# Two transformer-like MLP layers after an attention: the second layer's first product in a Strassen form

## The chip, the cores and the metric

One core of one Trainium2 chip. The metric is device time in microseconds (us) of one execution, as the median of a few executions. TensorE is PE in the rows, VectorE is DVE, ScalarE is ACT, GpSimd is POOL; SP is SyncE, which here only starts DMAs.

## The reference

```python
def _attn_ref(x, state):                                  # x 4x8x512x64, state 4x8x32x64
    a  = softmax(scale * x @ state.T);     xread = a @ state     # 512 tokens of each batch
    a2 = softmax(scale * state @ x.T);     sread = a2 @ x        # 32 state rows of each batch
    return np.concatenate([xread, sread], axis=2)
def _moe_ref(x, w_in, w_out):                             # layer 1: ELU
    h = x @ w_in                                          # 512 -> 2048
    return np.where(h > 0, h, np.exp(np.minimum(h, 0)) - 1) @ w_out   # 2048 -> 512
def _moe2_ref(x, w_in, w_out):                            # layer 2: mish
    h = x @ w_in
    sp = np.where(h > 20, h, np.log1p(np.exp(np.minimum(h, 20))))
    return (h * np.tanh(sp)) @ w_out
```

The attention gives 4·(512 + 32) = 2176 rows of 512, which both layers take one after the other. The weights come as 64-bit floats and are converted on the chip.

## The kernel before

**Precision.** A product is taken to float32 accuracy with three fast matmuls: each operand is split into a rounded high part and the rest (`copy` and a subtraction), and high·high, high·low and low·high are added in PSUM (L756 to L758, L836 to L838).

**Tokens.** 17 tiles of 128: four batches of four tiles, and a last tile with the 4·32 state rows. A *step* is one block of tokens and one block j of 128 of the 2048 features: its first product (`mm1`) fills a PSUM bank `h`, `hidden` makes g of it on ACT and DVE, and `mm2`, two steps later, multiplies g by w_out into accumulators `acc`. Layer 1 takes a batch (512 tokens) at a time, steps (1, b, j); its last batches add their second half of features to results that lie in DRAM as x2d, loaded again as `half` (L889), added, and written back (L896). Layer 2 has five blocks of 4, 4, 3, 3 and 3 tiles (`BLOCKS2`), steps (2, blk, j): 12 matmuls of n·128 columns, then n·3 of 512 columns.

**Mish** of a tile is a chain over two engines: exp on ACT (L775), minimum (L792) and u = e·(e+2) (L793) on DVE, Ln (L795) and exp (L796) on ACT, two products (L797, L798) on DVE, then the high part (L800, ACT) and the rest (L801, DVE).

**Weights of layer 2** are converted during layer 1 (L453 to L478), written to DRAM (`w2d`, L481), loaded again when layer 1 ends (`reload`), and split (L500). `load_x2` loads and splits a block of layer 2's input.

**Order.** `Plan` keeps a list of operations with costs, data dependences and due times, and fixes every engine's order before the kernel runs: each engine executes its list strictly in that order, each DMA too is started in the order of its queue's list. PSUM has the banks `h` (two), `att` (two) and `acc0` to `acc3`.

## Time and profile before

| | |
|---|---|
| median of 3 runs | 743.83 us (743.46 to 744.91) |
| the profiled execution: time, and its span in the trace | 744.95 us, 743.2 us |
| TensorE busy over the span | 723.5 us, 3874 matmuls |
| VectorE / ScalarE busy | 532.1 us / 448.0 us |
| share of the last chain that is TensorE's | 95% |
| start of layer 2's first matmul | 355.2 us |

The span is what the trace covers; the time of an execution is 1.75 us more. Matmuls overlap, so a matmul's own duration is longer than its share of the engine: what counts is the distance from one start to the next.

### The profile page before, as it was taken

How to read it: one execution, taken by the hardware profiler on the slowest of the kernel's cores; microseconds unless marked ns; L12 is line 12 of the kernel's file. 1: busy time of each engine (PE TensorE's matmuls, PEld its weight loads, DVE VectorE, ACT ScalarE, POOL GpSimd, SP SyncE). 2: the span in 40 equal slices, each digit the busy share in tenths (PEclk: the TensorE clock that was granted, in tenths of full speed). 3: DMA queues.
4: the chain of work that ended last, by engine and by line, in shares of the span. 5: the costliest groups of instructions: out<-in, count | busy, mean ns of one | idle time of the engine just before them, and what ended most of it. 6: DMA issues, size and time to landing. Idle time of an engine off the chain costs nothing.

```text
span 743.2 us, 10373 instructions
## 1 busy us (share of the span) xinstructions
PE 723.5 (97%) x3874; PEld 580.2 (78%) x3874; DVE 532.1 (72%) x955; ACT 448.0 (60%) x796; POOL 2.7 (0%) x14
## 2 busy tenths in 40 slices
PE   4899999999999999999999999999999999999996
PEld 3345777776777779878888888888899999989894
DVE  6889988768478884687899856575567566666553
ACT  4687787656388673777767645454545455555443
POOL 0000000000000000000000000000000000000000
...
GB/s 226 280 174 64 119 158 201 41 142 1 159 161 156 91 202 56 200 241 180 254 185 231 44 0 100 1 0 1 6 94 1 1 86 1 1 1 43 1 1 42
DMA packets 48090, 73.28 MB, mean 99 GB/s; under 512 B 5544, under 2 KB 28840, under 8 KB 48040
## 3 DMA queue, kind: packets, MB, share of 16 engines
...
q10 hardware_dynamic: 2212, 0.66, 0.4%
...
## 4 chain that ended last, share of the span: by engine, by line
PE 95%; DVE 2%; ACT 1%; DMA 1%; issue 0%; ACTq 0%
PE acc_acc L836 16%; PE acc_acc L838 15%; PE acc_acc L837 15%; PE h L756 12%; PE h L758 12%; PE h L757 12%; PE acc_acc L824 3%; PE h L742 2%; PE fold L535 2%; PE h L732 2%; DMA st_raw<-in_state 1%; PE xT L601 1%; PE sr L684 1%; PE acc_att L837 0%; PE acc_att L836 0%; PE acc_att L838 0%
## 5 line engine op out<-in xcount | busy, mean ns | idle before, releaser
L775 ACT ACTIVATE e<-h 128x512 f32<-128x512 f32 (+1 forms) x148 | 83.2, 562 | 129.6 <-PE h L758 117.9
L800 ACT CAST g<-e 128x512 fp32r<-128x512 f32 (+1 forms) x142 | 82.4, 580 | 61.7 <-PE acc_acc L838 31.6
L801 DVE TENSOR_TENSOR g<-e,g 128x512 fp32r<-128x512 f32 (+1 forms) x142 | 91.2, 642 | 28.7 <-ACT g L800 27.9
L838 PE MATMUL acc_acc<-w_out,g 128*128 128x512 f32 x272 | 106.9, 393 | 0.0
L837 PE MATMUL acc_acc<-w_out,g 128*128 128x512 f32 x272 | 106.7, 392 | 0.0
L836 PE MATMUL acc_acc<-w_out,g 128*128 128x512 f32 x272 | 105.9, 389 | 0.4 <-ACT g L800 0.4
L836 PE MATMUL acc_acc<-g,w_out 128*128 128x512 f32 x232 | 93.3, 402 | 0.0
L838 PE MATMUL acc_acc<-g,w_out 128*128 128x512 f32 x232 | 90.6, 391 | 0.0
L837 PE MATMUL acc_acc<-g,w_out 128*128 128x512 f32 x232 | 90.4, 390 | 0.0
L797 DVE TENSOR_TENSOR u<-u,e 128x384 f32<-128x384 f32 (+1 forms) x80 | 48.9, 611 | 54.0 <-ACT e L796 53.9
L795 ACT ACTIVATE e<-u,two 128x384 f32<-128x384 f32 (+1 forms) x80 | 52.8, 660 | 49.4 <-DVE u L793 49.3
L792 DVE TENSOR_SCALAR e<-e 128x384 f32<-128x384 f32 (+1 forms) x80 | 30.9, 386 | 51.6 <-ACT e L775 51.6
L785 DVE SCALAR_TENSOR_TENSOR e<-e,h 128x512 f32<-128x512 f32 x62 | 42.3, 683 | 27.3 <-ACT e L778 27.2
L838 PEld LDWEIGHTS acc_acc<-w_out,g 128*128 128x128 f32 x272 | 51.1, 188 | 11.0 <-DVE g L801 0.3
L836 PEld LDWEIGHTS acc_acc<-w_out,g 128*128 128x128 f32 x272 | 51.1, 188 | 10.1 <-ACT g L800 0.9
L837 PEld LDWEIGHTS acc_acc<-w_out,g 128*128 128x128 f32 x272 | 51.0, 188 | 9.5
L836 PEld LDWEIGHTS acc_acc<-g,w_out 128*128 128x128 f32 x232 | 43.6, 188 | 18.4 <-issue 6.3
L758 PE MATMUL h<-x,w_pair 128*128 128x384 f32 (+1 forms) x160 | 57.3, 358 | 0.0
L758 PE MATMUL h<-x,w_in 128*128 128x384 f32 (+1 forms) x160 | 57.3, 358 | 0.0
L756 PE MATMUL h<-x,w_pair 128*128 128x384 f32 (+1 forms) x160 | 57.3, 358 | 0.0
L756 PE MATMUL h<-x,w_in 128*128 128x384 f32 (+1 forms) x160 | 57.3, 358 | 0.0
L757 PE MATMUL h<-x,w_in 128*128 128x384 f32 (+1 forms) x160 | 57.2, 357 | 0.0
(135 smaller groups left out, 1324.1 us busy)
## 6 DMA issues: line engine op xcount, KB each, us to landing
raw_out<-in_moe_w_out SPq DMA_DIRECT2D x32, 512.0 KB, 3.8
raw_in<-in_moe_w_in SPq DMA_DIRECT2D x32, 256.0 KB, 5.9
raw_in<-in_moe_w_in SPq DMA_DIRECT2D x16, 512.0 KB, 4.1
w2d<-wv SPq DMA_DIRECT2D x32, 256.0 KB, 3.0
xb<-in_x SPq DMA_DIRECT2D x16, 256.0 KB, 5.2
x2d<-o SPq DMA_DIRECT2D x16, 256.0 KB, 3.9
back_in<-w2d SPq DMA_DIRECT2D x16, 256.0 KB, 2.8
back_out<-w2d SPq DMA_DIRECT2D x16, 256.0 KB, 2.9
```

The costliest lines, as they stand in the source:

```text
L756: nc.tensor.matmul(h[:, :n], lhsT=wh, rhs=xh, start=(k == 0), stop=False)
L757: nc.tensor.matmul(h[:, :n], lhsT=wh, rhs=xl, start=False, stop=False)
L758: nc.tensor.matmul(h[:, :n], lhsT=wl, rhs=xh, start=False, stop=(k == nk - 1))
L775: add("ACT", act(n), lambda: nc.scalar.activation(E(), Hh(), AF.Exp), r=[h], w=[e])
L785: add("DVE", dve(n), lambda: nc.vector.scalar_tensor_tensor(E(), E(), -1.0, Hh(), ALU.mult, ALU.max), r=[e, h], w=[e])
L795: add("ACT", act(n) + 0.12, lambda: nc.scalar.activation(E(), U(), AF.Ln, bias=two), r=[u, "two"], w=[e])
L797: add("DVE", dve(n), lambda: nc.vector.tensor_tensor(U(), U(), E(), ALU.mult), r=[u, e], w=[u])
L800: add("ACT", act(n) + 0.01, lambda: nc.scalar.copy(g[:, 0, :n], E()), r=[e], w=[(g, 0)])
L801: add("DVE", dve(n), lambda: nc.vector.tensor_tensor(g[:, 1, :n], E(), g[:, 0, :n].bitcast(F32), ALU.subtract), r=[e, (g, 0)], w=[(g, 1)])
L836: nc.tensor.matmul(acc.t, lhsT=st[:, 0, :], rhs=mv[:, 0, :], start=fst, stop=False)
L837: nc.tensor.matmul(acc.t, lhsT=st[:, 0, :], rhs=mv[:, 1, :], start=False, stop=False)
L838: nc.tensor.matmul(acc.t, lhsT=st[:, 1, :], rhs=mv[:, 0, :], start=False, stop=lst)
```

## The change

Layer 2's 16 full tiles are taken in two halves m of 1024 tokens, and the features in eight pairs p of blocks. In each the first product is a 2×2×2 product of half-blocks (512 tokens, 128 features, 256 of the depth) in Strassen-Winograd form: seven half-block products of 6 matmuls of 512 columns (`product`, L1009 of the changed kernel), instead of eight. It needs

- sums of halves of w_in2 (`combine`, in layer 1: per pair four half-width sums, four high parts, four rests, eight DMAs to `wi2d`), loaded per pair (`load_pair`);
- four sums of layer 2's input and seven splits (`load_x2`), once per half;
- per pair three copies of a PSUM bank to SBUF on ACT (`out_of`, L1021: p1, u2, u3), and three sums of such a copy and a bank on DVE (`plus`: c11, and the two late blocks).

Of a pair's four blocks (two of features, two of 512 tokens) the two of the first 512 tokens get their mish and second product at once. The two of the second 512 tokens wait in SBUF as `late`; their mish follows the pair's own (for pairs 5 to 7 all together behind pair 7), and their second product comes after the pairs, 16 blocks at 12 matmuls. The state rows (last tile) lose their own block: in each pair of the second half, 12 matmuls of 256 columns (`last_tokens`), and later 16 transposes and 48 matmuls. w_out2 is converted at the end of layer 1 and in the first pairs of layer 2 (`last_weight`) and no longer goes through DRAM. The loads of `half` now come after the first product of the step in which they are placed, and the first products are chained in their order.

```diff
-BLOCKS2 = [(0, 4), (4, 4), (8, 3), (11, 3), (14, 3)]
+NP = NF // 2
+EITHER_LATE = 0.5
+BEHIND = 0.0
+PUT_OFF = 5
...
-    w2d = pools["dram"].tile([P, 2, NF, DM], F32, name="w2d")
+    wi2d = pools["dram"].tile([P, NP, 4, 2, 2, 2 * P], F32, name="wi2d")
...
+    def last_weight(j):
+        raw = buf("work", "wraw", 3, [P, DM], I64, f"raw_out2_{j}_")
+        y = buf("work", "wy", 2, [P, DM], F32, f"last_y{j}_")
+        v = buf("work", "wv", 2, [P, DM], F32, f"last_v{j}_")
+        r = lambda i: raw.t.bitcast(U32).rearrange("p (f t) -> p f t", t=2)[:, :, i]
+        add(SP, 512.0, lambda: nc.sync.dma_start(out=raw.t, in_=w_dram[2][1][j * P:(j + 1) * P, :]), w=[raw],
...
+    def combine(p, a1, a2):
+        tt(lambda: sb[:, lo], lambda: a2[:, lo], lambda: a2[:, hi], ALU.add, [a2], [(sb, 0)])
+        tt(lambda: sa[:, lo], lambda: sb[:, lo], lambda: a1[:, lo], ALU.subtract, [a1, (sb, 0)], [(sa, 0)])
+        tt(lambda: sa[:, hi], lambda: a1[:, lo], lambda: a2[:, lo], ALU.subtract, [a1, a2], [(sa, 1)])
+        tt(lambda: sb[:, hi], lambda: a1[:, hi], lambda: sa[:, lo], ALU.subtract, [a1, (sa, 0)], [(sb, 1)])
...
+        for i, v in enumerate((a1, a2, sa, sb)):
+            r = [v] if i < 2 else [(v, 0), (v, 1)]
+            h, l = (buf("work", "o", OBUFS, [P, DM], F32R, f"comb{p}_{i}_{q}_") for q in range(2))
+            add(EITHER, {"ACT": 0.61, "DVE": 0.43}, lambda e, v=v, h=h: copy(e, h.t, v.t), r=r, w=[h], place=[l])
+            add("DVE", 0.69, lambda v=v, h=h, l=l: nc.vector.tensor_tensor(l.t, v.t, h.t.bitcast(F32), ALU.subtract),
+                r=[*r, h], w=[l])
+            for q, t in enumerate((h, l)):
+                add(SP, 256.0, lambda i=i, q=q, t=t: nc.sync.dma_start(
+                    out=wi2d[:, p, i // 2 * 2:i // 2 * 2 + 2, i % 2, q, :], in_=t.t.bitcast(F32).rearrange("p (s f) -> p s f", s=2)),
+                    r=[t], w=[("wi2d", p, i, q)])
...
+                add(SP, 256.0, lambda o=o, rows=rows: nc.sync.dma_start(out=o.t, in_=rows), r=names, w=[o], lag=2.0,
+                    after=[step_op[s]])
...
+        load("b12", 0, 1)
+        load("b11", 0, 0)
+        load("b22", 1, 1)
+        load("b21", 1, 0)
+        minus("t1", "b12", "b11")
+        split("b11")
+        minus("t2", "b22", "t1")
+        minus("t3", "b22", "b12")
+        split("t1")
+        minus("t4", "b21", "t2")
+        split("b21")
+        split("t2")
+        split("t4")
+        split("t3")
+        split("b22")
+        x2_done[:] = [plan.writer[sums["t4"]]]
...
+    def load_pair(m, p):
+        pair_t[m, p] = [buf("w", "w_in", NF // 2, [P, 2, 2, 2 * P], F32R, f"pair{m}_{p}_{i}_") for i in range(4)]
+        for i, t in enumerate(pair_t[m, p]):
+            n = (m * NP + p) * 4 + i
+            add(SP, 512.0, lambda i=i, t=t: nc.sync.dma_start(out=t.t.bitcast(F32), in_=wi2d[:, p, i]),
+                             r=[("wi2d", p, i // 2 * 2 + g, q) for g in range(2) for q in range(2)], w=[t], lag=1.0,
+                after=[last_use[n - 6]] if n >= 6 else x2_done if n >= 4 else folded)
+
+
+    PRODUCTS = [(0, 0, "b11"), (1, 0, "b21"), (2, 0, "t2"), (2, 1, "t1"), (3, 0, "t3"), (1, 1, "t4"), (3, 1, "b22")]
+
+    put_off = []
...
+    def mish(H, keys, dst, wkeys, after=()):
+
+
+        e = buf("work", "e", EBUFS, [P, MAXN])
+        u = buf("work", "vu", 2, [P, MAXN], F32, "u")
+        add("ACT", act(S), lambda: nc.scalar.activation(e.t, H(), AF.Exp), r=keys, w=[e], after=after)
+        add("DVE", 0.43, lambda: nc.vector.tensor_scalar(e.t, e.t, E20, None, ALU.min), r=[e], w=[e])
+        add("DVE", 0.69, lambda: nc.vector.scalar_tensor_tensor(u.t, e.t, 2.0, e.t, ALU.add, ALU.mult), r=[e], w=[u])
+        add("ACT", act(S) + 0.12, lambda: nc.scalar.activation(e.t, u.t, AF.Ln, bias=two), r=[u, "two"], w=[e])
+        add("ACT", act(S) + 0.03, lambda: nc.scalar.activation(e.t, e.t, AF.Exp, scale=-1.0), r=[e], w=[e])
+        add("DVE", 0.69, lambda: nc.vector.tensor_tensor(u.t, u.t, e.t, ALU.mult), r=[u, e], w=[u])
+        if dst is None:
+            add("DVE", 0.69, lambda: nc.vector.tensor_tensor(e.t, H(), u.t, ALU.mult), r=[*keys, u], w=[e])
+            return high_low(lambda: e.t, [e])
+        add("DVE", 0.69, lambda: nc.vector.tensor_tensor(dst(), H(), u.t, ALU.mult), r=[*keys, u], w=wkeys)
+
+    def high_low(src, keys):
+        g = buf("work", "g", GBUFS, [P, 2, MAXN], F32R, "g")
+        turn_[:] = [add("ACT", act(S), lambda: nc.scalar.copy(g[:, 0, :], src()), r=keys, w=[(g, 0)], after=turn_)]
+        add("DVE", 0.69, lambda: nc.vector.tensor_tensor(
+            g[:, 1, :], src(), g[:, 0, :].bitcast(F32), ALU.subtract), r=[*keys, (g, 0)], w=[(g, 1)])
+        return g
+    def pair(m, p, due, late):
...
+        ps = [buf("ps", t, 2, [P, MAXN], F32, f"prod{m}_{p}_") for t in ("h", "att", "att")]
...
+        def product(q, bank, fst, lst):
+            n, pos, name = PRODUCTS[q]
+            w, x = parts[n], X[name]
+
+            def f():
+                for k in range(2):
+                    c = slice(k * P, (k + 1) * P)
+                    for i, (a, b) in enumerate(((0, 0), (0, 1), (1, 0))):
+                        nc.tensor.matmul(bank.t, lhsT=w[:, pos, a, c], rhs=x[b][:, k, :],
+                                         start=fst and k == i == 0, stop=lst and k == 1 and i == 2,
+                                         skip_group_check=not fst)
+
+            chain[:] = [add("PE", 6 * mm(S), f, r=[w, part(x[0], 0), part(x[1], 0)], w=[bank],
+                            due=due[q], after=chain)]
+            last_use[(m * NP + p) * 4 + n] = chain[0]
+
+        def plus(o, a, bank, r, w):
+            add("DVE", 0.69, lambda: nc.vector.tensor_tensor(o(), a.t, bank.t, ALU.add), r=[a, bank, *r], w=w)
+
+        def out_of(o, bank):
+            add("ACT", act(S), lambda: nc.scalar.copy(o.t, bank.t), r=[bank], w=[o], after=converted)
+
+        end = p == NP - 1
+        product(0, ps[0], True, True)
+        out_of(P1S, ps[0])
+        product(1, ps[1], True, True)
+        plus(lambda: C11.t, P1S, ps[1], [], [C11])
+        product(2, ps[0], False, True)
+        out_of(U2, ps[0])
+        if m:
+            last_tokens(p, due[7])
+        if not end:
+            product(3, ps[2], True, True)
+        product(4, ps[0], False, True)
+        out_of(U3, ps[0])
+        if end:
+            product(5, ps[0], False, True)
+            product(3, ps[2], True, True)
+        plus(lambda: L(1), U3, ps[2], [], [B_[1]])
+        if not end:
+            product(5, ps[0], False, True)
+        product(6, ps[2], False, True)
+        plus(lambda: L(0), U2, ps[2], [], [B_[0]])
+        g = [mish(lambda: C11.t, [C11], None, None), mish(lambda: ps[0].t, [ps[0]], None, None)]
+        for e in range(2):
+            put_off.append((L, e, B_[e]))
+        if p < PUT_OFF or end:
+            first = chain if end else ()
+            for L, e, b in put_off:
+                mish(lambda e=e, L=L: L(e), [b], lambda e=e, L=L: L(e), [b], after=first)
+            put_off.clear()
+        return g
...
+        for m in range(2):
...
+                todo = [[p, e, i, 0.0] for e in range(2) for i in range(NC)]
+            moved[m] = chain[0]
+            if not m:
+                load_x2(1)
+                load_x16()
+            block = 2 * NC * m
+            for i in range(NC):
+                for e in range(2):
+                    d = tick(C3)
+                    out_mm(g[NP - 1][e], NF - 2 + e, slice(i * P, (i + 1) * P), A_(i), False, e == 1, d)
+                result(block + i, A_(i), d, 0)
+            if m:
+                last_out(tick)
+            accB = [buf("ps", t, 2, [P, MAXN], F32, f"accB{m}_{i}_") for i, t in enumerate(("att", "att", "h", "h"))]
+            gB = [None] * NF
+            for j in range(NF):
+                gB[j] = high_low(lambda t=late[m, j]: t[0][:, t[1], :], [late[m, j]])
+                if j < NF - 2:
+                    for i in range(NC):
+                        out_mm(gB[j], j, slice(i * P, (i + 1) * P), accB[i], j == 0, False, tick(C3), chain)
+            for n, i in enumerate((2, 3, 0, 1)):
+                for j in (NF - 2, NF - 1):
+                    d = tick(C3)
+                    out_mm(gB[j], j, slice(i * P, (i + 1) * P), accB[i], False, j == NF - 1, d)
+                if not n:
+                    chain[:] = [plan.ops[-1]]
+                result(block + NC + i, accB[i], d, 0 if not m else 2 if n == NC - 1 else 1)
...
+    def last_tokens(p, due):
...
+        def f():
+            for k in range(NK):
+                w, c = halves[k // 2], slice(k % 2 * P, (k % 2 + 1) * P)
+                for i, (a, b) in enumerate(((0, 0), (0, 1), (1, 0))):
+                    nc.tensor.matmul(bank[:, :2 * P].rearrange("p (s f) -> p s f", s=2), lhsT=t[:, a, k, :],
+                                     rhs=w[:, :, b, c], start=k == i == 0, stop=k == NK - 1 and i == 2)
+
+        chain[:] = [add("PE", 12 * mm(2 * P), f, r=[(t, 0), (t, 1), *halves], w=[bank], due=due, after=chain)]
...
     for j in range(NF):
+        begin(min(index[1, 3, j] + 2, first2 - 1), last_weight, j)
+    for j in range(NF):
         begin(GATE_SECOND + 2 * j, weight, "in", 2, j)
-        begin(GATE_SECOND + 2 * j + 1, weight, "out", 2, j)
-    for j in range(NF):
-        begin(index[1, 3, j], reload, "in", j)
-        begin(min(index[1, 3, j] + 1, first2), reload, "out", j)
-    for blk in range(len(BLOCKS2)):
-        begin(first2 + NF * (blk - 1) + 6 if blk else s_state + NQ + 4, load_x2, blk)
+    begin(s_state + NQ + 4, load_x2, 0)
+    begin(s_state + NQ + 4, load_pair, 0, 0)
...
     assert not later
+    second_layer()
```

TensorE's order at the end of the first pair. Before: a step's end and the next second product (`acc`); after: the products of pair 0, where prod_0_822 and prod_0_824 are banks (of the tags `h` and `att`).

```order
L758 MATMUL h_768_3687<-x_0_0_691_3264,w_pair_660_3091 128x512
L756 MATMUL h_768_3687<-x_0_0_691_3264,w_pair_660_3091 128x512
L757 MATMUL h_768_3687<-x_0_1_692_3272,w_pair_660_3091 128x512
L758 MATMUL h_768_3687<-x_0_0_691_3264,w_pair_660_3091 128x512
L836 MATMUL acc_0_acc_760_3608<-w_out_2_634_2927,g_3675 128x512 [waits Activation_49]
L837 MATMUL acc_0_acc_760_3608<-w_out_2_634_2927,g_3675 128x512
L838 MATMUL acc_0_acc_760_3608<-w_out_2_634_2927,g_3675 128x512 [waits DVE_49]
```

```order
L1009 MATMUL prod_0_824_3770<-x_0_t_0_740_3535,pair_0_2_752_3520 128x512
L1009 MATMUL prod_0_822_3685<-x_0_t_742_3416,pair_0_3_753_3540 128x512 [waits DMAHW3_49,Activation_49]
L1009 MATMUL prod_0_822_3685<-x_0_t_742_3416,pair_0_3_753_3540 128x512 x5
L1009 MATMUL prod_0_822_3685<-x_0_t_743_3679,pair_0_1_751_3500 128x512 [waits Activation_49]
L1009 MATMUL prod_0_822_3685<-x_0_t_743_3679,pair_0_1_751_3500 128x512 x5
L1009 MATMUL prod_0_824_3770<-x_0_b_0_744_3542,pair_0_3_753_3540 128x512 [waits DVE_49]
L1009 MATMUL prod_0_824_3770<-x_0_b_1_745_3457,pair_0_3_753_3540 128x512
L1009 MATMUL prod_1_843_3828<-x_0_b_0_734_3511,pair_1_0_835_3663 128x512 [waits DMAHW0_49]
```

Where second products stood between first products, the products of pair 0 now follow each other, and two that add to the same bank stand one behind the other with ScalarE's copy of that bank between them.

ScalarE's order, in a 4-tile block of layer 2 before, and around pair 1 after.

```order
L796 ACTIVATE e_4349<-e_4349 128x512 [waits Activation_49]
L800 CAST g_4386<-e_4349 128x512 [waits DVE_49,PE_49]
L775 ACTIVATE e_4391<-h_839_4370 128x512 [waits PE_49]
L795 ACTIVATE e_4391<-u_4401,two 128x512 [waits DVE_49]
L796 ACTIVATE e_4391<-e_4391 128x512 [waits Activation_49]
L800 CAST g_4426<-e_4391 128x512 [waits DVE_49,PE_49]
```

```order
L972 ACTIVATE e_3854<-u_3863,two 128x512 [waits DVE_49]
L973 ACTIVATE e_3854<-e_3854 128x512 [waits Activation_49]
L295 CAST w_out_10_781_3892<-last_v_773_3821 128x512 [waits DVE_49]
L973 ACTIVATE e_3810<-e_3810 128x512
L982 CAST g_3913<-e_3854 128x512 [waits DVE_49]
L1021 COPY u__0_1_841_3916<-prod_1_843_3828 128x512 [waits DVE_49,PE_49]
L969 ACTIVATE e_3919<-c__0_1_842_3898 128x512 [waits DVE_49]
L969 ACTIVATE e_3927<-late_0_821_3807 128x512 [waits DVE_49]
L1021 COPY u__0_1_840_3934<-prod_1_843_3828 128x512 [waits PE_49]
```

Between the activations of one mish there now stand the copies of banks (u2 and u3 of pair 1), a weight's cast and the activations of a second mish.

SyncE's list of DMAs near the end of layer 1, around the loads of `half`.

```order
L889 DMA half_0_491_1569<-x2d 128x512 [waits DMAHW2_49]
L889 DMA half_1_492_1576<-x2d 128x512 [waits DMAHW3_49]
L896 DMA x2d<-half_3_401_1560 128x512 [waits DMAHW4_49,DVE_49]
L889 DMA half_2_493_1644<-x2d 128x512 [waits DMAHW7_49]
L561 DMA xb_1928<-in_x 128x2x256 [waits PE_49]
```

```order
L540 DMA wi2d<-comb_2_0_367_2079 128x2x256 [waits DMAHW6_49,Activation_49]
L880 DMA half_1_522_2100<-x2d 128x512 [waits DMAHW7_49,DMAHW3_49]
L540 DMA wi2d<-comb_2_1_368_2080 128x2x256 [waits DMAHW0_49,DVE_49]
L880 DMA half_2_523_2121<-x2d 128x512 [waits DMAHW1_49,Activation_49]
L540 DMA wi2d<-comb_3_0_369_2123 128x2x256 [waits DMAHW2_49,Activation_49]
L540 DMA wi2d<-comb_3_1_370_2124 128x2x256 [waits DVE_49]
L880 DMA half_3_524_2160<-x2d 128x512 [waits DMAHW4_49,Activation_49]
L887 DMA x2d<-half_1_522_2100 128x512 [waits DMAHW7_49,DMAHW5_49,DVE_49]
```

The loads of `half` stood close together; they now stand between writes of `comb` that wait for ScalarE and VectorE.

## Rows read from the trace of the kernel before

**Rows 1.** The page's first part: busy time, share, instructions of each engine

```profile
PE 723.5 (97%) x3874; PEld 580.2 (78%) x3874; DVE 532.1 (72%) x955; ACT 448.0 (60%) x796; POOL 2.7 (0%) x14
```

**Rows 2.** The page's chain that ended last, by engine

```profile
PE 95%; DVE 2%; ACT 1%; DMA 1%; issue 0%; ACTq 0%
```

**Rows 3.** Windows: stretch, length, engines' busy time (count), clock, DMA share, GB/s

```profile
core 0: us, PE busy (x) PEld busy (x) DVE busy (x) ACT busy (x) POOL busy (x), PEclk, DMA share, GB/s
0.00:50.00 50.00, 37.63 (x204) 18.09 (x205) 38.69 (x76) 32.30 (x62) 0.31 (x6) 0.86 0.95 239
50.00:355.20 305.20, 304.83 (x1872) 231.62 (x1871) 237.04 (x411) 210.34 (x362) 2.34 (x8) 1.00 0.43 135
355.20:529.30 174.10, 174.10 (x770) 144.23 (x769) 125.71 (x208) 100.61 (x168) 0.00 (x0) 1.00 0.27 85
529.30:731.00 201.70, 201.70 (x1013) 182.76 (x1012) 127.12 (x255) 102.01 (x201) 0.00 (x0) 1.00 0.07 22
731.00:743.20 12.20, 5.24 (x22) 3.47 (x20) 3.57 (x8) 2.77 (x6) 0.00 (x0) 0.88 0.20 64
```

**Rows 4.** Timeline of TensorE, first matmuls of two successive steps of four tiles

```profile
366.04 0.39 PE L756 MATMUL h<-x,w_in 128*128 128x512 f32 x1
...
371.48 0.39 PE L756 MATMUL h<-x,w_in 128*128 128x512 f32 x1
```

**Rows 5.** Timeline of TensorE, one step of three tiles

```profile
601.77 0.33 PE L756 MATMUL h<-x,w_in 128*128 128x384 f32 x1
...
603.88 0.39 PE L836 MATMUL acc_acc<-w_out,g 128*128 128x512 f32 x1
...
605.96 0.33 PE L756 MATMUL h<-x,w_in 128*128 128x384 f32 x1
```

**Rows 6.** Timeline of TensorE, 32 matmuls of 128 columns in layer 1

```profile
277.96 3.73 PE L732 MATMUL h<-sread,w 128*128 128x128 f32 x32
281.45 0.48 PE L836 MATMUL acc_acc<-g,w_out 128*128 128x512 f32 x1
```

**Rows 7.** Timeline of ScalarE and TensorE around the end of a first product

```profile
194.43 0.39 PE L758 MATMUL h<-x,m 128*128 128x512 f32 x1
...
194.86 0.60 ACT L775 ACTIVATE e<-h 128x512 f32<-128x512 f32 x1 [0.74 <-PE h L758]
```

**Rows 8.** Timeline of VectorE: two independent, then two dependent instructions; minimum

```profile
420.83 0.69 DVE L500 TENSOR_TENSOR w_out<-back_out,w_out 128x512 fp32r<-128x512 f32 x1
421.43 0.68 DVE L797 TENSOR_TENSOR u<-u,e 128x512 f32<-128x512 f32 x1
422.15 0.69 DVE L798 TENSOR_TENSOR e<-h,u 128x512 f32<-128x512 f32 x1
...
358.71 0.43 DVE L792 TENSOR_SCALAR e<-e 128x512 f32<-128x512 f32 x1 [0.80 <-ACT e L775]
359.17 0.69 DVE L793 SCALAR_TENSOR_TENSOR u<-e 128x512 f32<-128x512 f32 x1
```

**Rows 9.** ScalarE: a group of copies out of PSUM; timeline of two activations

```profile
L289 ACT COPY o<-acc_acc 128x512 f32<-128x512 f32 x21 | 12.2, 587 | 1.8 <-PE acc_acc L838 0.7
...
358.57 0.66 ACT L453 ACTIVATE wy<-raw_out 128x512 f32<-128x512 f32 x1
359.14 0.67 ACT L455 ACTIVATE wv<-raw_out 128x512 uint32<-128x512 uint32 x1
```

**Rows 10.** Waits inside mish: total us, times, longest us

```profile
DVE u L797 <- ACT e L796: 53.9, 62, 1.5
DVE e L792 <- ACT e L775: 51.6, 63, 1.4
```

**Rows 11.** DMA issues of `half`: count, KB, median us from issue to landing

```profile
half<-x2d SPq DMA_DIRECT2D x8, 256.0 KB, 2.8
```

**Rows 12.** Windows of the start and of the very end

```profile
10.00:20.00 10.00, 2.54 (x33) 0.70 (x32) 9.37 (x20) 6.64 (x15) 0.00 (x0) 0.66 1.12 240
...
733.00:735.00 2.00, 1.56 (x7) 0.81 (x6) 1.11 (x2) 0.51 (x1) 0.00 (x0) 1.00 0.00 0
```

More of the change, by code (lines that the diff above doesn't have):

```diff
@@ L183, in run @@
             (t, _, _), op, e = best
+            if e == "DVE" and len(op.engs) > 1 and free[e] > 80.0:
+                t -= EITHER_LATE
             if e == "PE" and self.filler:
@@ L429, in weight @@
         v = buf("work", "wv", 2, [P, DM], F32, "wv")
+        to2 = buf("work", "vu", 2, [P, DM], F32, "vp") if (kind, layer) == ("in", 2) else v
         def load():
@@ L503, in reload @@
-    def reload(kind, j):
-        v = buf("work", "wraw", 3, [P, DM], F32, f"back_{kind}_{j}_")
-        add(SP, 256.0, lambda: nc.sync.dma_start(out=v.t, in_=w2d[:, kind == "out", j, :]),
-            r=[("w2d", kind, j)], w=[v])
-        split_weight(kind, 2, j, v)
-    m_sb, m_hl = {}, {}
+        w = w_sb[kind, layer, j] = buf("w", f"w_{kind}", NF, [P, 2, DM], F32R, f"w_{kind}{layer}_{j}_")
+        add(EITHER, {"ACT": 0.61, "DVE": 0.43}, lambda e: copy(e, w[:, 0, :], v.t), r=[v], w=[(w, 0)])
@@ new lines, in hidden @@
+        add("ACT", act(n) + 0.12, lambda: nc.scalar.activation(E(), E(), AF.Relu, bias=one, scale=-1.0),
+            r=[e, "one"], w=[e])
+        if whole_out(kind, blk, j):
+            g = gs[s] = buf("work", "g", GBUFS, [P, MAXN], F32, "gw")
+            add("DVE", dve(n), lambda: nc.vector.scalar_tensor_tensor(
+                g.t, E(), -1.0, Hh(), ALU.mult, ALU.max), r=[e, h], w=[g])
+            return
+        add("DVE", dve(n), lambda: nc.vector.scalar_tensor_tensor(E(), E(), -1.0, Hh(), ALU.mult, ALU.max),
+            r=[e, h], w=[e])
@@ L906, in load_x2 @@
[L906 to L920 removed]
+            add(SP, 256.0, lambda o=o, rows=rows: nc.sync.dma_start(out=rows, in_=o.t), r=[o], w=names,
+                due=due + 4.0)
@@ new lines, in attention_elu_mish, with load_x16 @@
+    x16, g16 = [], []
+    def load_x16():
+        raw = buf("work", "o", OBUFS, [P, NK, P], F32, "x16raw")
+        t = buf("work", "wraw", 3, [P, 2, NK, P], F32R, "x16_")
+        x16.append(t)
+        add(SP, 256.0, lambda: nc.sync.dma_start(out=raw.t, in_=x2d[:, :, (NT - 1) * P:]),
+            r=[("x2d", NT - 1, i) for i in range(NK)], w=[raw], after=[moved[0]])
+        add(EITHER, {"ACT": act(S), "DVE": 0.43}, lambda e: copy(e, t[:, 0], raw.t), r=[raw], w=[(t, 0)])
+        add("DVE", 0.69, lambda: nc.vector.tensor_tensor(
+            t[:, 1], raw.t, t[:, 0].bitcast(F32), ALU.subtract), r=[raw, (t, 0)], w=[(t, 1)])
@@ new lines, in last_tokens, with f @@
+    def last_tokens(p, due):
+        t, halves = x16[0], pair_t[1, p][:2]
+        bank = buf("ps", "att", 2, [P, MAXN], F32, f"h16_{p}_")
+        if p % 4 == 0:
+            g16.append(buf("work", "wraw", 3, [P, 2, S], F32, f"g16_{p}_"))
+        G, half, part = g16[-1], p % 4 // 2, p % 2
+        def f():
+            for k in range(NK):
[4 more added lines that the diff above has]
+        chain[:] = [add("PE", 12 * mm(2 * P), f, r=[(t, 0), (t, 1), *halves], w=[bank], due=due, after=chain)]
+        last_use[(NP + p) * 4] = chain[0]
+        add(EITHER, both(2 * P), lambda e: copy(e, G[:, half, part * 2 * P:(part + 1) * 2 * P], bank[:, :2 * P]),
+            r=[bank], w=[(G, half, part)])
+        if part:
+            keys = [(G, half, 0), (G, half, 1)]
+            mish(lambda: G[:, half], keys, lambda: G[:, half], keys)
@@ new lines, in last_out, with turn @@
+    def last_out(tick):
+        acc = buf("ps", "acc0", 1, [P, MAXN], F32, "acc16_")
+        for n in range(NC):
+            G, half = g16[n // 2], n % 2
+            pt = buf("ps", f"acc{1 + n % 3}", 1, [P, MAXN], F32, f"turn16_{n}_")
+            def turn(G=G, half=half, pt=pt):
+                for i in range(NC):
+                    nc.tensor.transpose(pt[:, i * P:(i + 1) * P], G[:, half, i * P:(i + 1) * P], ident)
+            add("PE", NC * 0.11, turn, r=["ident", (G, half, 0), (G, half, 1)], w=[pt], due=tick(NC * 0.11) - 4.0)
+            g = high_low(lambda pt=pt: pt.t, [pt])
+            for i in range(NC):
+                j = NC * n + i
+                d = tick(C3_)
+                out_mm(g, j, slice(i * P, (i + 1) * P), acc, j == 0, j == NF - 1, d)
+        result(NT - 1, acc, d, 0)
```

285 lines of the change are left out of this document (159 added, 126 removed).

## The prediction

> **What bounds the kernel now.** I read the busy times first: TensorE works in 723.5 of 743.2 us [rows 1], and the chain that ended last is 95% TensorE [rows 2]. The windows by stage then show where there is slack: TensorE is full from 50 to 731 us, in layer 1 (305 us, 0.4 us free) and in layer 2 (174.10 and 201.70 us, nothing free), always at a granted clock of 1.00 [rows 3]. VectorE has 237.04 of 305.20 us in layer 1, 72% in layer 2's four-tile blocks, 63% in the three-tile ones; ScalarE less. So TensorE's matmul count sets the time, and each us of other work is free as long as no matmul waits for it.
>
> The pace comes from distances between starts. A four-tile step of 24 matmuls of 512 columns takes 371.48 − 366.04 = 5.44 us, 0.2267 each [rows 4]. A three-tile step takes 4.19: twelve of 384 columns in 2.11 (0.176 each) and nine of 512 in 2.08 (0.231) [rows 5]. 128 columns take (281.45 − 277.96)/32 = 0.109 [rows 6].
>
> **What TensorE saves.** Before, layer 2 is 32 steps of 5.44 and 48 of 4.19: 375.2 us, against 375.8 in the two windows [rows 3]. After:
> - first product, 2 halves × 8 pairs × 7 products × 6 = 672 matmuls of 512 columns: 152.3 us;
> - second product, 17 tiles × 16 blocks × 3 = 816: 185.0;
> - the state rows' first product, 96 of 256 columns. No row has 256; between 0.109 (128 columns) and 0.176 (384), that is 10.5 to 16.9 us. From 384 to 512 columns a matmul grows by about 0.051 per 128, so I take 0.125: 12.0 us;
> - 16 transposes at 0.109: 1.7.
>
> Sum 351.0, so TensorE saves 24.2 us (19.3 to 25.7 by the bound of the 256 columns). Without full three-tile blocks the shorter matmuls, dearer per column, go too; that is most of the gain beyond the eighth of the first product. At the end 0.44 us without matmuls (2.00 − 1.56 in the window 733 to 735) go away, because several accumulators end in turn [rows 12].
>
> *A rule that speaks against the size.* By the rows, 512 columns cost 226.7 ns and 384 cost 176. The Trainium skill (TensorE: Matmul & The Clock Gate, section "Back-to-back issue gap") gives the isolated gap between matmuls as columns divided by 2.4 GHz plus 2.5 ns, which is 215.8, 162.5 and 109 ns for 512, 384 and 256. By these figures the saving would be 20.1 us, an estimate from that page, and the forecast 4 us later. The trace does not agree with the figures, so the rows' own pace stays in the sum.
>
> **Work that moves to other engines in layer 1.** The sums of w_in2 add to VectorE 32 half-width operations (at most 0.46, the minimum's distance) and 32 rests (0.60, independent instructions) [rows 8]: 34 us, less the splits of w_out that move out. Added to 38.69 + 237.04 [rows 3] this leaves VectorE below 310 of 355 us. ScalarE gets up to 32 casts of 0.57 (activations 358.57 to 359.14 [rows 9]), 18 us on 243 of 355. Neither becomes full, so I price this work at nothing, with TensorE's matmuls as its cover. If the cover fails it is through waits in a queue:
>
> *The change of batch.* The loads of `half` now stand in SyncE's list between the writes of `comb`, each of which waits for a cast on ScalarE or a rest on VectorE. Behind SyncE's waiting write stand the next loads, behind these the sums that free the accumulators, behind these the next batch's second products. The last load after batch 1 leaves some four writes after the first one; at a cast or rest of 0.6 each with one other instruction of 0.6 in front, 4 × 1.2 = 4.8. Then 2.8 to land [rows 11] and 0.7 for the sum (the dependent distance of [rows 8]): 8.3 us. TensorE has 24 matmuls left in that time, 5.4. A wait of 2.9 us follows (0 to 8.3). For the other changes of batch, whose lists I did not walk, 1.1 (0 to 3).
>
> **Waits that the pairs add in layer 2.** A bank that is used twice in a pair must be copied first. A copy of 512 columns takes 0.59 us [rows 9] and starts 0.2 after the matmul's pace ends (194.43 + 0.23 against 194.86 [rows 7]): 0.8 us, which one product between (6 × 0.2267 = 1.36) covers unless ScalarE is busy with something that waits.
> - Pair 0, first half: two products of the same bank follow each other, nothing covers the copy u3, and an activation of about 0.6 may stand before it: 1.4.
> - Pair 1: the copy u2 is listed behind a cast of g that waits for VectorE, two dependent products of 0.72 [rows 8], then the cast (0.6), the copy (0.6) and the 0.2: near 3.0, less one product: 1.6.
> - Pairs 3 and 4, and pair 0 of the second half, where one instruction stands before a copy: 0.7, 0.8 and 1.0.
> - The other eleven pairs have the same shape and I did not walk them. Between nothing (one product covers 0.8) and 0.9 each (an activation and a VectorE instruction in front) I take 0.4, since copies mostly meet a free ScalarE (58 and 51% busy in layer 2 [rows 3]): 4.4 (0 to 9.9).
> - Turning the state rows' g before their second product: a copy and a transpose, 0.7 uncovered.
>
> VectorE is the other thing to watch. In pairs 1 to 4 of the first half it must do 81 instructions (mish of four blocks a pair, three sums, the conversion of w_out2): 70 at 0.60 and 11 at 0.46, with 20 dependent ones that add 0.12 each [rows 8]: 49.5 us, for 216 matmuls or 48.9 us of TensorE. That is full. In pairs 5 to 7 two mish of each pair are put off, so the load falls; in the late blocks behind them it rises again to nearly full. I price this overload at the 0.6 us that it exceeds, within the waits above, since second products can fill in.
>
> **Sum.** Waits: 2.9 + 1.1 + 1.4 + 1.6 + 2.5 + 4.4 + 0.7 = 14.6. The profiled run (744.95, span 743.2) stands 1.1 above the median of 743.83, and its stages are the same matmuls, so the difference is put on the median: −24.2 − 0.4 + 14.6 = −10.0, 733.8 us.
>
> **Rivals.**
> - *All copies covered.* If ScalarE is free at each copy and the loads of `half` come in time, only a few of the 14.6 stay: 720 to 727. For it: ScalarE's 51 to 58% in layer 2. Against: its list is strict, and a wait of one instruction delays the copy behind it.
> - *VectorE sets the pace of pairs 0 to 4 (slower).* Mish waits already today inside its chain: 53.9 + 51.6 us over the 80 functions of layer 2, 1.3 each [rows 10]. These are hidden because other steps are in flight. If in the stretch where VectorE is full each of 20 functions keeps these 1.3 us in TensorE's way, that is 26 us in place of the 4.5 walked there: some 756. It turns the change into a loss from about 10 us more than I take, 0.5 per function. For it: 49.5 against 48.9. Against: today's VectorE is 72% busy in layer 2 and TensorE loses nothing.
> - *Layer 1's queue eats the gain (no change).* If the loads of `half` wait 4 to 5 us at each of the three late changes of batch, near 8.3 at worst, the gain is gone: about 743. Against: the accumulators are freed one at a time, and the first load stands early.
> - *The clock drops.* TensorE starts at the lower of its two levels (1.2 GHz against 2.4), with 0.66 granted on average from 10 to 20 us, while it works 2.54 of 10 us; after that it stays at 1.00 even with the 0.44 us gap of the end [rows 12]. Every us of matmuls at the lower level costs another; 10 us of work there cancel the gain, and a fifth of the pairs' 152.3 us would give 764. The Trainium skill (TensorE: Matmul & The Clock Gate, section "A second HAM failure mode: psum-queue depth-cycling") reports a kernel whose short idles between groups of matmuls let the clock oscillate. By that rule the pairs with a wait each would run partly at the lower level. The trace of before has no such gaps inside layer 2, so it neither shows nor excludes it; one short gap, at the end, did no harm.
>
> **How the numbers follow.** The forecast (728 to 741, some waits in most pairs) 0.61; all covered 0.18; VectorE full 0.10; layer 1's queue 0.08; the clock 0.03. The likeliest time is 733.8. Low end: the waits that I did not walk at nothing and half of the walked ones stay, with the saving's upper bound, 743.8 − 25.7 − 0.4 + 5 = 723; I give 725, which leaves out the lower half of the second case (0.09). High end: 745, which takes in the layer-1 case and leaves out VectorE and the clock (0.13 less a part that stays below). A measurement here tells 0.2%, 1.5 us, from no change. Faster by more than that: the forecast, the covered case and a small part of the others, 0.80; within it 0.08, mostly the layer-1 case; slower 0.12.
>
> **What would show it.** In the changed profile: TensorE's matmuls in layer 2 worth 351 us at 0.227 apart, and 0.125 for the 256-column ones (0.109 would give 1.5 us more, 0.176 take 4.9). A share of TensorE's idle time in layer 2 of about 10 us, ended by ScalarE's copies (u2, u3) at the places named, and about 4 us at the changes of batch, ended by the sums of `half`. The clock at 1.00 in all windows past 50 us. VectorE over 95% busy in pairs 1 to 4. Wrong would be: waits ended by VectorE's g or c11 of over 10 us in the first half (the VectorE rival), a first product of the second layer that starts later than 356 us by more than the waits at the batches, or a window below 1.00 in layer 2.

## The result: 2.6% faster

The changed kernel takes 725.4 us (724.48 to 728.63, 4 runs) against 744.21: ratio 0.9755, interval 0.9723 to 0.9788. Run again: 725.26 against 744.12, ratio 0.9744 (0.9731 to 0.9758), so 18.9 us less, 0.3 us above the low end of the stated range and outside the forecast's own 728 to 741. The profiled executions differ by more, 20.7 us of span; the account below is made on these.

First the page of the changed kernel: busy times, and the chain that ended last.

```profile
PE 700.7 (97%) x3698; PEld 545.5 (76%) x3698; DVE 568.6 (79%) x957; ACT 494.2 (68%) x853; POOL 3.0 (0%) x14
...
PE 91%; DVE 5%; ACT 2%; DMA 1%; issue 1%; ACTq 0%; DVEq 0%
```

Against [rows 1, 2] TensorE has 22.8 us less and is still the chain, but 4% of the chain has gone to other engines. The windows by stage (columns as in [rows 3]) show where:

```profile
0.00:50.00 50.00, 38.52 (x218) 17.93 (x219) 39.58 (x79) 33.80 (x63) 0.32 (x6) 0.90 0.90 232
50.00:356.70 306.70, 303.93 (x1858) 231.22 (x1857) 257.61 (x443) 233.82 (x410) 2.65 (x8) 1.00 0.55 171
356.70:538.00 181.30, 178.22 (x787) 146.24 (x785) 147.97 (x233) 123.48 (x206) 0.00 (x0) 1.00 0.47 151
538.00:664.00 126.00, 125.30 (x597) 105.08 (x598) 98.63 (x164) 82.57 (x143) 0.00 (x0) 1.00 0.38 111
664.00:710.00 46.00, 46.00 (x206) 38.09 (x205) 21.68 (x35) 17.79 (x30) 0.00 (x0) 1.00 0.04 11
710.00:722.40 12.40, 8.75 (x39) 6.92 (x37) 3.08 (x6) 2.74 (x6) 0.00 (x0) 1.00 0.26 85
```

Layer 2 starts at 356.70 in place of 355.20; up to 538 us it has 3.1 us without matmuls, from there to 664 us 0.7; the clock is 1.00 in every stage past 50 us. TensorE's timeline names all waits over 0.3 us after 50 us (in brackets: idle time, and who ended it):

```profile
70.75 0.50 PE L846 MATMUL acc_acc<-g,w_out 128*128 128x512 f32 x1 [1.46 <-DVE w_out L499]
205.49 0.50 PE L844 MATMUL acc_acc<-g,w_out 128*128 128x512 f32 x1 [0.50 <-DVE half L882]
208.23 0.66 PE L637 MATMUL xT<-ident,xb 128*128 128x128 f32 x4 [0.52 <-ACT raw L295]
370.12 1.66 PE L1009 MATMUL prod<-x_t,pair 128*128 128x512 f32 x6 [1.00 <-ACT u__0_0_818_3798 L1021]
382.25 1.65 PE L1009 MATMUL prod<-x_t,pair 128*128 128x512 f32 x6 [0.94 <-ACT u__0_1_841_3916 L1021]
425.52 1.66 PE L1009 MATMUL prod<-x_t,pair 128*128 128x512 f32 x6 [0.61 <-ACT u__0_4_909_4314 L1021]
538.15 1.66 PE L1009 MATMUL prod<-x_t,pair 128*128 128x512 f32 x6 [0.68 <-ACT u__1_0_1040_5237 L1021]
663.66 0.66 PE L1192 MATMUL turn<-ident,g 128*128 128x128 f32 x4 [0.55 <-DVE g L983]
```

These are the places that the forecast walked (pairs 0, 1, 4, pair 0 of the second half, the turn), and no others in layer 2. A wait costs some 0.3 us more than its bracket, by the distances of starts: the group before that of 370.12 starts at 366.22 and has 12 matmuls, 2.72 us, so it costs 370.12 − 366.22 − 2.72 = 1.18, and the matmuls behind it are 0.14 late as well. Summed in this way layer 2 waits 5.6 us.

| us | forecast | profiled execution |
|---|---|---|
| layer 2's matmuls | −24.2 | −24.2 |
| gap at the end of before | −0.4 | −0.8 |
| waits in layer 2 | +10.6 | +5.6 |
| layer 1 | +4.0 | +1.5 |
| from last matmul's start to the end | 0 | −2.8 |
| sum | −10.0 | −20.7 |

The matmuls' line: from 356.70 to the last start at 718.36 and one pace more are 361.9 us; without 24 matmuls of layer 1 that still follow (5.4) and the 5.6 of waits, 350.9. Before it was 381.3, less 5.4 and the gap at the end: 375.1. That gap is a wait of 0.44 us at 734.20 and the late starts behind it, 0.8 in all by distances. The last line: before, the last matmul starts at 736.29 and the span ends 6.9 us later; now 4.1 us later.

The line of layer 1 depends on the execution. Layer 2 starts between 354.2 and 355.2 us in three traces with the old layer 1, and between 356.5 and 359.0 in nine with the new one: 2.8 us later on average. The differences arise in the first 50 us, and this pair of traces is a favourable one: that is most of why it gives 20.7 where the medians give 18.9.

### The profile page after: what moved, and what is told of

Same layout as the page of the kernel before. It is cut to its first block, busy times and chain, and to the rows that moved or that the text cites. A ratio compares the mean times of both kernels' runs of the same rounds, so it can differ in the third digit from the quotient of the medians.

```text
span 722.4 us, 10157 instructions
## 1 busy us (share of the span) xinstructions
PE 700.7 (97%) x3698; PEld 545.5 (76%) x3698; DVE 568.6 (79%) x957; ACT 494.2 (68%) x853; POOL 3.0 (0%) x14
## 4 chain that ended last, share of the span: by engine, by line
PE 91%; DVE 5%; ACT 2%; DMA 1%; issue 1%; ACTq 0%; DVEq 0%
PE prod L1009 20%; PE acc_acc L844 7%; PE acc_acc L846 7%; PE acc_acc L845 7%; PE accB L1060 4%; PE accB L1059 4%; PE accB L1058 4%; PE h L787 4%; PE accA L1058 4%; PE accA L1059 4%; PE accA L1060 4%; PE h L789 4%; PE h L788 3%; PE acc_acc L837 3%; PE h L778 2%; PE fold L570 2%
## 5 line engine op out<-in xcount | busy, mean ns | idle before, releaser
L1009 PE MATMUL prod<-x_t,pair 128*128 128x512 f32 x384 | 97.3, 391 | 3.2 <-ACT u__0_0_818_3798 L1021 1.0
L1009 PEld LDWEIGHTS prod<-x_t,pair 128*128 128x128 f32 x384 | 71.6, 188 | 20.0 <-ACT u__0_0_818_3798 L1021 1.4
L1009 PE MATMUL prod<-x_b,pair 128*128 128x512 f32 x288 | 71.5, 389 | 0.0
L972 ACT ACTIVATE e<-u,two 128x512 f32<-128x512 f32 x68 | 49.1, 722 | 21.5 <-DVE u L971 21.4
L1009 PEld LDWEIGHTS prod<-x_b,pair 128*128 128x128 f32 x288 | 54.1, 188 | 11.3
L974 DVE TENSOR_TENSOR u<-u,e 128x512 f32<-128x512 f32 x68 | 46.7, 687 | 15.1 <-ACT e L973 14.4
L844 PEld LDWEIGHTS acc_acc<-g,w_out 128*128 128x128 f32 x232 | 43.6, 188 | 19.3 <-issue 7.5
L846 PEld LDWEIGHTS acc_acc<-g,w_out 128*128 128x128 f32 x232 | 43.5, 188 | 11.1 <-DVE w_out L499 1.9
L803 ACT ACTIVATE e<-e,one 128x512 f32<-128x512 f32 x68 | 49.3, 725 | 1.9
L845 PEld LDWEIGHTS acc_acc<-g,w_out 128*128 128x128 f32 x232 | 43.6, 188 | 8.9 <-DVE g L814 0.4
L1060 PE MATMUL accA<-w_out,g 128*128 128x512 f32 x128 | 49.9, 390 | 0.0
L1058 PE MATMUL accA<-w_out,g 128*128 128x512 f32 x128 | 49.9, 390 | 0.0
L1059 PE MATMUL accA<-w_out,g 128*128 128x512 f32 x128 | 49.9, 390 | 0.0
L1058 PE MATMUL accB<-w_out,g 128*128 128x512 f32 x128 | 49.8, 389 | 0.0
L1059 PE MATMUL accB<-w_out,g 128*128 128x512 f32 x128 | 49.8, 389 | 0.0
```

The lines of the kernel that those rows point to most:

```text
L803: add("ACT", act(n) + 0.12, lambda: nc.scalar.activation(E(), E(), AF.Relu, bias=one, scale=-1.0), r=[e, "one"], w=[e])
L844: nc.tensor.matmul(acc.t, lhsT=st[:, 0, :], rhs=mv[:, 0, :], start=fst, stop=False)
L845: nc.tensor.matmul(acc.t, lhsT=st[:, 0, :], rhs=mv[:, 1, :], start=False, stop=False)
L846: nc.tensor.matmul(acc.t, lhsT=st[:, 1, :], rhs=mv[:, 0, :], start=False, stop=lst)
L972: add("ACT", act(S) + 0.12, lambda: nc.scalar.activation(e.t, u.t, AF.Ln, bias=two), r=[u, "two"], w=[e])
L974: add("DVE", 0.69, lambda: nc.vector.tensor_tensor(u.t, u.t, e.t, ALU.mult), r=[u, e], w=[u])
```

## The experiments

The changed kernel was run again beside the eighth product and the first two kernels of the tail; the differences to 725.26 of all others are between groups, in which the kernel before takes 744.12, 744.36 and 744.45. For differences near 1 us the traces tell more: from layer 2's first product to the last matmul the changed kernel takes 361.66 and, run again, 361.63 us.

**What the products are worth.** One product of each pair made twice, so eight per pair:

```diff
-                for k in range(2):
+                for k in (0, 1, 0, 1) if q == 1 else range(2):
```

> The changed kernel with the second product of each pair made twice (the same 6 matmuls into the same bank, started anew), so that a pair has eight products. Theory (TensorE's count sets the time): 16 times 1.36 us = 21.8 us more, less at most 3 us of waits for copies that the extra matmuls may cover, so 743 to 747 us. Rival (much of the gain comes from elsewhere, and the extra products fall into waits of VectorE): under 15 us more, below 740.

Measured 750.37, 25.1 over the changed kernel run beside it and 0.8% (0.7 to 1.0) slower than the kernel before. The 96 matmuls account for 21.8 of it, and layer 2 loses 2.7 more (from first product to last matmul 386.05 against 361.63): they did not cover the copies, as I had thought. Its longest wait, and the window right behind it (columns as in [rows 3], clock 0.50):

```profile
373.08 2.37 PE L1009 MATMUL prod<-x_t,pair 128*128 128x512 f32 x6 [2.68 <-ACT u__0_0_819_3808 L1021]
...
373.80:377.10 3.30, 3.30 (x10) 2.51 (x9) 2.15 (x4) 1.75 (x4) 0.00 (x0) 0.50 0.41 149
```

The place is still pair 0, but the copy is u2 and not u3; ScalarE's list has another order there. Behind this wait TensorE runs at the lower level for a while, with matmuls 0.43 us apart in place of 0.227: 1.6 of the 2.7 us. Without the eighth product saved the change would lose.

**The tail.** Three kernels. In the kernel before, the tiles of the last block in reverse order (`order = order[::-1]`), so that the state rows come first:

> The kernel before, with the three tiles of its last block finished in reverse order, so that the state rows are written out before the last two tiles and not last. Theory (2.9 us of the gain are a shorter tail, because the write of the state rows used only part of the DMA engines): about 741 us, with some 4 us from the last matmul to the end in place of 6.9. Rival (the tail is shorter because the last accumulators end 1.4 us apart): within 0.5 us of the kernel before.

Measured 744.45 against 744.12, ratio 1.0003 (0.9994 to 1.0012): nothing. Next, the changed kernel with that write behind all others:

```diff
+            if c == NT - 1:
+                held.append((o, to))
+                return
...
+        add(SP, 256.0, lambda: nc.sync.dma_start(out=to, in_=o.t), r=[o], after=last_op, due=d + 4.0)
```

> The changed kernel, with the write of the state rows held back until the last tile's result is there; nothing else moves. Theory of the tail: 2 to 3 us slower than the changed kernel, 727 to 728. Rival: the same as the changed kernel.

Measured 729.9: 4.6 more than the changed kernel, and more than the 2 to 3 expected. From the last matmul to the end its trace has 8.6 us in place of 4.1; the held write goes out in one piece behind all others, where the kernel before writes the state rows in two halves. And the kernel before with the block of the state rows moved ahead:

```diff
-BLOCKS2 = [(0, 4), (4, 4), (8, 3), (11, 3), (14, 3)]
+BLOCKS2 = [(0, 4), (4, 4), (14, 3), (8, 3), (11, 3)]
```

> The kernel before, with its last block of three tiles (14 to 16, with the state rows) moved two blocks ahead, so that the state rows are written some 130 us before the end. Theory of the tail: the write of the state rows, slow on part of the DMA engines, ends the run in the kernel before; here from the last matmul to the end some 4 us in place of 6.9, about 741.3 us. Rival: the tail stays at 6.9, within 0.5 us of the kernel before.

Measured 741.8 against 744.36, ratio 0.9965 (0.9952 to 0.9977): 2.6 less. The DMA view of the last 8 us (busy tenths and GB/s in 40 slices) shows why, first of the kernel before, whose last write is the state rows:

```profile
DMA  0000001987949779422222222222222200000000
GB/s 0 0 0 0 0 0 41 338 261 236 343 154 333 256 230 348 123 26 46 82 77 87 77 92 82 102 97 87 102 102 92 92 26 0 0 0 0 0 0 0
```

and of the kernel with the block moved ahead, where it is a plain tile:

```profile
DMA  0000000000000000007959689699999300000000
GB/s 0 0 0 0 0 0 0 0 0 0 0 0 0 0 0 0 0 0 241 333 174 338 220 297 307 210 343 338 364 328 343 98 0 0 0 0 0 0 0 0
```

The write of the state rows (32 rows of each batch) keeps the DMA engines at 2 tenths and moves 80 to 100 GB/s, plain tiles at some 300. The reversal failed because it gave the write 1.4 us of lead where it needs about 5: in its trace DMA ends as late as before. With the block moved ahead, the tail is 4.6 us in place of 6.9. So 2.3 of the 2.8 us come from the state rows' new place, not from the seven products, and the kernel before could have had them; what the other 0.5 are is not shown.

**The rule on the loads of `half`**, taken out:

```diff
-                add(SP, 256.0, lambda o=o, rows=rows: nc.sync.dma_start(out=o.t, in_=rows), r=names, w=[o], lag=2.0,
-                    after=[step_op[s]])
+                add(SP, 256.0, lambda o=o, rows=rows: nc.sync.dma_start(out=o.t, in_=rows), r=names, w=[o], lag=2.0)
```

> The changed kernel without the rule that the loads of half come after the step's first product. Theory of the forecast (the loads stand between waiting writes, and the batch change waits for them): the 0.5 us wait of TensorE behind the sum of half at the change after batch 1 goes away, 0.5 to 1.5 us less than the changed kernel. Rival (the wait comes from the order of layer 1 as a whole, which the rule sets): layer 1 gets other waits, 1 to 5 us more.

Measured 753.93, 28.7 over the changed kernel: neither theory had the size, and mine had the sign wrong. The wait behind `half` did go away, and layer 2 starts at 354.66. Then:

```profile
378.53 6.91 PE L1008 MATMUL prod<-x_t,pair 128*128 128x512 f32 x18 [15.55 <-ACT p__0_0_817_3662 L1020]
```

The copy p1 stands on ScalarE behind casts for `comb`, and comes after the last sums of w_in2, which are late: DVE's last rest of them (L537) starts at 379.03, in the changed kernel run again at 328.37. SyncE's list shows where the time went, here without the rule, loads of `half`, their write back, and the first raw block of w_in2:

```profile
158.89 0.32 SPq L880 DMA_DIRECT2D half<-x2d  x1
192.06 1.51 SPq L886 DMA_DIRECT2D x2d<-half  x3
...
195.31 0.99 SPq L444 DMA_DIRECT2D raw_in<-in_moe_w_in  x2
```

and with it:

```profile
129.47 5.07 SPq L444 DMA_DIRECT2D raw_in<-in_moe_w_in  x2
...
188.04 0.33 SPq L880 DMA_DIRECT2D half<-x2d  x1
192.75 0.34 SPq L887 DMA_DIRECT2D x2d<-half  x1
```

`half` and the raw weights share the tag `wraw` with three buffers. Loaded at 158.89 and not at 188.04, `half` holds them until 192, the conversion of w_in2 begins 66 us later, and its end moves into layer 2. That the shared buffers do this is read from these rows; a separate buffer for `half` was not tried. The windows of this run also show the clock:

```profile
350.00:360.00 10.00, 10.00 (x46) 8.29 (x45) 7.05 (x11) 6.09 (x9) 0.00 (x0) 1.00 0.69 221
360.00:370.00 10.00, 2.98 (x14) 2.13 (x12) 9.90 (x13) 5.28 (x10) 0.00 (x0) 0.81 0.77 259
370.00:380.00 10.00, 1.47 (x4) 1.20 (x5) 3.45 (x7) 3.63 (x7) 0.00 (x0) 0.50 0.81 272
380.00:390.00 10.00, 9.27 (x33) 6.85 (x32) 7.98 (x14) 5.65 (x10) 0.00 (x0) 0.83 0.78 230
```

In the long idle it falls to 0.50, the lower level, and the next 10 us, full of matmuls again, still have 0.83 on average; the waits of up to 1.46 us in the changed kernel leave it at 1.00.

**The waits of the pairs.** The first product of pair 1 between the two of pair 0 that share a bank:

```diff
+        if not p:
+            load_pair(m, 1)
+            ahead[m, 1] = buf("ps", "h", 2, [P, MAXN], F32, f"prod{m}_1_")
+            product(0, ahead[m, 1], True, True, 1)
         if not end:
             product(5, ps[0], False, True)
```

> The changed kernel with the first product of pair 1 put between the two products of pair 0 that need the same bank, in both halves. Theory (TensorE waits there for the copy of the bank alone, with nothing between): the waits of 1.0 and 0.7 us in pair 0 go away, 1 to 2 us less than the changed kernel. Rival (ScalarE and VectorE are late as a whole, and the wait comes back at the next copy or at the first second product of pair 1): no change within 0.5 us, with waits of the same sum in pair 1.

Measured 726.79, 1.5 more than the changed kernel; from first product to last matmul 362.65 against 361.63. The waits for copies in pairs 0, 1 and 4 and in the second half's pair 0 are all gone, and in their place stands mainly one at pair 1's first second product, again with the clock at 0.50 behind it:

```profile
383.00 0.50 PE L1066 MATMUL accA<-w_out,g 128*128 128x512 f32 x1 [1.56 <-ACT g L982]
...
384.40:387.70 3.30, 3.30 (x9) 2.43 (x9) 2.87 (x6) 2.00 (x4) 0.00 (x0) 0.50 0.03 10
```

So the rival in part: the wait comes back at pair 1, behind the chain of mish. But the loss is the clock's: the matmuls of that stretch are 0.43 us apart, which costs 1.6 us, more than the 1.0 lost. Without it, by this count, the edit would have been worth some 0.6 us: four short waits did no harm to the clock, one longer wait did. Copies that may go to VectorE:

```diff
-            add("ACT", act(S), lambda: nc.scalar.copy(o.t, bank.t), r=[bank], w=[o], after=converted)
+            add(EITHER, both(S), lambda e: copy(e, o.t, bank.t), r=[bank], w=[o], after=converted)
```

> The changed kernel, with the copies p1, u2 and u3 free to go to VectorE or ScalarE, as the order's planner finds. Theory of the forecast (a copy is late because it is listed on ScalarE behind an instruction that waits): the waits of about 1 us at pairs 0, 1 and 4 change places or shrink, 0 to 1.5 us less than the changed kernel. Rival (VectorE is the fuller engine, at 90% in the first half's pairs, so a copy that goes there costs more): 1 to 4 us more.

Measured 728.68, 3.4 more: the rival. TensorE now waits for g (0.79, 0.61 us) beside copies (0.90, 0.78).

**VectorE's room.** `plus(C11)` made four times in each pair (`for _ in range(4):`):

> The changed kernel with the sum c11 made four times in each pair: 48 instructions or some 30 us more on VectorE in the pairs, nothing on the other engines. Theory of the forecast (VectorE is full in pairs 0 to 4 of the first half, so each us more there is paid): 15 extra instructions in those five pairs, 9 to 10 us, reach the time almost whole: 6 us or more above the changed kernel. Rival (VectorE has some 10% free there, and waits come only from single copies): 1 to 4 us more.

Measured 738.64, 13.4 more for 48 instructions. The first half's pairs (first product to the first matmul into accB) take 140.1 us in place of 128.8, so 11.3 is paid there for 24 instructions, and pairs 2 to 5 have two waits each like these, with brackets of 1.4 us together:

```profile
419.72 1.66 PE L1009 MATMUL prod<-x_t,pair 128*128 128x512 f32 x6 [0.21 <-ACT u__0_3_888_4223 L1021]
422.52 1.67 PE L1009 MATMUL prod<-x_t,pair 128*128 128x512 f32 x6 [1.15 <-ACT u__0_3_887_4241 L1021]
```

By starts, these four pairs take 68.25 us in place of 60.96: 7.3 us for twelve instructions of 0.69, or 8.3. Nearly all of each instruction is paid; the room is about 0.25 us a pair, and the 0.6 in an expectation below came from the brackets alone. The added sums also stand in front of c11's own mish, and this run does not tell that delay from the full engine. The other way, one instruction of each w_out2 block left out (`for by, op in ((0x80000000, ALU.bitwise_and),):`):

> The changed kernel without one of the two instructions that put each block of w_out2 together (its exponent's lower bits are left out, so the result is not the reference's): 16 instructions, some 11 us, less on VectorE, half of them in pairs 0 to 3. Theory (VectorE at about 90% still leaves no wait of its own, the few waits are single copies behind single instructions): 0 to 1.5 us less than the changed kernel. Rival (VectorE sets the pace of these pairs): 3 us less or more, with the waits of the first half's pairs gone.

Measured 725.12, 0.1 less (from first product to last matmul 361.53). VectorE in the first stretch of the pairs, in the changed kernel and here:

```profile
357.00:431.00 74.00, 71.45 (x312) 57.94 (x311) 66.71 (x110) 55.62 (x96) 0.00 (x0) 1.00 0.58 202
```

```profile
357.00:431.00 74.00, 71.51 (x312) 57.93 (x311) 62.52 (x103) 57.51 (x100) 0.00 (x0) 1.00 0.59 198
```

Four us less on VectorE, and TensorE as busy as before: its waits, 0.67, 0.68 and 1.14 us, now stand in pairs 0 to 2. So VectorE's work just about fits under TensorE's: less of it gains nothing, more of it is mostly paid. Last, no mish put off (`PUT_OFF = 8`):

> The changed kernel with no mish put off: pairs 5 to 7 too make the mish of their late blocks at once, 5 more per half in the pairs and 5 less after them. Theory (VectorE has about 0.6 us free in a pair before a wait comes, and a pair with four mish is full): pairs 5 to 7 take 0.5 to 1.5 us more each in the first half, the late blocks have nothing to lose: 1 to 4 us more than the changed kernel. Rival (VectorE has enough room in pairs 5 to 7): no change within 0.5 us.

Measured 726.23, 1.0 more (ratios 0.9763, 0.9749 to 0.9776, and 0.9744, 0.9731 to 0.9758: not told apart by the times). From first product to last matmul it takes 362.76 us, 1.1 more, which speaks for the theory at its low end. Its trace has one new pair of waits, 0.54 and 0.49 us behind g at 486 us, and lacks that of the turn.

**Layer 1's chain of first products** taken out (`after=[step_op[s - 1]]` in three places):

> The changed kernel without the rule that layer 1's first products follow each other in their order. Theory (the wait of 1.4 us at 71 us, behind a rest of w_out, comes from the chain of first products, which keeps TensorE's list from the order it had): it goes away, 1 to 1.5 us less. Rival (it comes from the order on VectorE, where the buffers of w1 are dealt otherwise): no change within 0.5 us.

Measured 725.94, no change. The wait at 71 us halves to 0.78, and 0.40 and 0.30 appear elsewhere; layer 2 starts at 357.44 against 357.45. Neither theory is shown; whose order causes that wait stays open.

## Why the prediction was right, and too small

- **The case**: the time lies in the rival of covered copies (720 to 727, 0.18), not in the forecast's 728 to 741 (0.61). The range holds it because its low end took in half of that rival, and by a tail that was not foreseen: without its 2.8 us the changed kernel would stand near 728. Most terms that were off were off in one direction.
- **The saving**, 24.2 forecast and 24.2 found. The 256-column matmuls took 0.120 us (12 in 1.44), forecast 0.125. The bound of 0.109 for 128 columns was misread: those rows of L732 are 16 matmuls of unsplit float32 that the trace shows as 32, so they give no price for a split matmul. The pace of 512 columns stayed at 0.227, so the gap that the Trainium skill gives (TensorE: Matmul & The Clock Gate, section "Back-to-back issue gap", 215.8 ns by its formula) is not this kernel's.
- **The walked waits** were right in place, and at pairs 0 and 1 in mechanism. At pair 1 the copy u2 stood behind the cast of g, which waited 1.57 us for a product on VectorE, as forecast:

```profile
380.96 0.62 ACT L982 CAST g<-e 128x512 fp32r<-128x512 f32 x1 [1.57 <-DVE e L976]
381.62 0.59 ACT L1021 COPY u__0_1_841_3916<-prod 128x512 f32<-128x512 f32 x1
```

  Counted by starts, pairs 0, 1, 3, 4 and the second half's pair 0 cost 1.3, 1.2, 0.2, 0.9 and 1.0 against 1.4, 1.6, 0.7, 0.8 and 1.0. At the last two and at the turn the price was right and the reason was not, which is luck. In pair 4 the copy u2 waited for the buffer that it writes, which a product on VectorE (L976) still read; in pair 0 of the second half u3 met a free ScalarE and simply had nothing between the two products:

```profile
424.89 0.59 ACT L1021 COPY u__0_4_909_4314<-prod 128x512 f32<-128x512 f32 x1 [0.56 <-DVE e L976]
537.51 0.59 ACT L1021 COPY u__1_0_1040_5237<-prod 128x512 f32<-128x512 f32 x1 [1.08 <-PE prod L1009]
585.70 0.59 ACT L1021 COPY u__1_3_1115_5677<-prod 128x512 f32<-128x512 f32 x1 [1.22 <-PE prod L1009]
```

  The turn waited 0.55 us for VectorE's rest of an earlier g, which frees the bank, and not for a copy and a transpose.
- **The pairs not walked, the step that failed most**: 4.4 forecast, nothing found, the largest error in the waits. A product or second products stand between there and cover the 0.8 us of a copy, and ScalarE was mostly free: the last row above is such a copy, for which ScalarE itself waited. I had taken a middle value between my bounds where the lower one held.
- **Layer 1**: 4.0 forecast, 1.5 found in this pair of traces and 2.8 on average, mostly for another reason. The change after batch 1 cost 0.5 where I had 2.9, since its loads left SyncE from 187 to 204 us, most of them in time; the other changes, priced at 1.1, show no wait behind a sum of `half`. The waits of 1.46 at 71 us and of 0.52 at 208 us (behind a copy on ScalarE) were not foreseen.
- **The tail**: 0 forecast, −2.8 found. I read that the state rows lose their own block, and only priced their matmuls; that their slow write no longer stands last is the term that was missing, 2.3 of the 2.8.
- **VectorE full**: I gave it 0.10. From the start of pair 1 to that of pair 5 (373.00 to 432.49) there are 253 matmuls, where I counted 216, and VectorE was busy for 55.8 of 59.5 us: 94%, just under the 95% that I named as a sign. So it had slightly more room than my 49.5 against 48.9, but little: 24 instructions more already cost 11.3 us, and the rival was near.
- **The clock**: waits of 0.55 to 1.00 us, five of them in layer 2, left it at 1.00 in every stage past 50 us. I gave this rival 0.03, and it was nearer than that: in two variants one wait of 1.56 and one of 2.68 us were each followed by a stretch at 0.50. The Trainium skill (TensorE: Matmul & The Clock Gate, section "A second HAM failure mode: psum-queue depth-cycling") tells of short idles that let it oscillate; no run here shows that, only single falls behind a longer wait.
